# Neighbourhood attention, first steps: order of GpSimd's sorts, a half tile filled by ScalarE, and a 384-column pass for V

## The chip, the cores and the metric

The kernel runs on one core of a Trainium2 chip. The metric is the device time of one execution in microseconds (us); a kernel's time is the median of its runs. In the profile PE is TensorE's matmul stream and PEld its weight loads, DVE is VectorE, ACT is ScalarE, POOL is GpSimd and SP is SyncE, which here only issues DMAs. L12 is line 12 of the kernel.

## The reference

The image is 224 x 224 pixels of 192 channels in bf16. Every pixel attends to a 7 x 7 window with a distance of 2 between neighbours, clipped at the borders:

```python
qkv = x @ wqkv
q, k, v = (qkv[..., :C], qkv[..., C:2 * C], qkv[..., 2 * C:])
...
logits = jnp.einsum('bnc,bnkc->bnk', qf, kn) * C ** (-0.5)   # kn: the 49 neighbours' keys
p = _softmax(logits, axis=-1)
o = jnp.einsum('bnk,bnkc->bnc', p, vn) @ wo
```

Because of the distance of 2, pixels of odd and even rows never meet, nor do those of odd and even columns: there are two row classes (rc 0 and 1) and two column classes (cc 0 and 1), each 112 pixels long.

## The kernel before

**Tiling.** There are 14 steps: 7 blocks of 16 rows (ti) by 2 row classes (rc), the class changing fastest. Step n has 7 pairs m of two slots, and a slot is 8 columns wide. So there are 98 pairs k, and the main loop runs over k. Key and query weights are multiplied together once (tiles aw), and so are value and output weights (tiles wp); the kernel then needs only two projections of x:

- G = x times aw, one "whole" item per column class and group of slots, and one "halves" item per group. ScalarE copies the latter out of PSUM as gx, and POOL copies gx into the second half of G (L456).
- V = x times wp, one V item per slot: `v_item` (L343), and `v_first` (L358) for seven items of row class 1 at the very start. An item is `v_mms` (L336): the 192 columns of each column class get a first pass over 128 channels and a second over the other 64, and each pass is two matmuls of 64 stationary columns (h = 0 and 1, which run side by side in the two column halves of the array). That is eight matmuls of 192 columns, with eight weight loads. The second pass of both classes reads the same stationary operand, at(1, h).

**Input.** x comes in 14 bands of 16 image rows. SP loads each band with three transposing DMAs (L154): k = 0 and k = 2 go to XA, k = 1 to a tile x1 of which there are two buffers, so the load of band 2's x1 waits until all readers of band 0's are done. Two copies (xb_items, L160) move x1 into XB, and three (sort_items, L170) rearrange a band into the tile XS, from which the V items read. In the start VectorE does the copies of bands 0 and 1 (L366, L160, L170), POOL the sort of band 1; later bands are copied by POOL. The V items made in step 1 (for step 2) need the sort of band 3, those made in step 2 that of band 4.

**A pair** runs through stage1 (scores s, L497; row maximum nmx on VectorE, L499), stage1b (exp on ScalarE, p, L507), stage2 (transposes of p on TensorE, L526, copied out by VectorE, pt_sb, L527), stage3 (o_ps = p times V, L536) and stage4 (VectorE divides by the row sum, L542 and L559, and DMAs go out). Stages 3 and 4 are those of the pair two before. V lies in two tiles: VF, and VD, which has the partition halves swapped and is filled from VF by DMAs (vd_high, vd_low). In step 0 the lower half of VD[0] meets only weights that are zero, so what it holds need only be finite.

**The order.** The order of each engine's instructions is that of the program (in_order, L89). Between the pairs' stages the main loop puts the next step's G items (gw, gh) and V items (vs). In step 0 it also has to finish step 0's own: the lists in L658 give each pair's items, and L703 says which of them VectorE copies out instead of ScalarE. POOL has a queue pool_q: the sorts and xb copies of a coming band are put at its head in given pairs (L727 to L738), DMAs that write the first slot's result (L588, fifteen or ten for a step) are appended at its end, and each pair takes four entries from it (pool_do, L748). POOL's gx copies and the out DMA in L569 are issued where they stand, so they come before that pair's four entries. In step 0 the sort of band 3 for class 0 is put in at pair 5; in step 1 that of band 4 for class 1 at pair 4.

Of the kernel before, what the change touches and what calls it, by code (L numbers as in the profile page):

```python
# [8 lines left out]
BF = mybir.dt.bfloat16  # L9
# [12 lines left out]
NSLOT = 14  # L22
NSTEP = 14
NBAND = 14
RP = 48
RW = 2 * S
MM = 16
BND = 16 * S
C = 192
# [69 lines left out]
def kernel(  # L99
# [189 lines left out]
    LAY = {(0, 0): (0, 128, 0), (0, 1): (128, 64, 0), (1, 0): (64, 128, 0), (1, 1): (0, 64, 64)}  # L289
    AW, WP = {}, {}  # L290
    for key, (c0, cn, p0) in LAY.items():
        AW[key] = pers.tile([128, C], BF, name="aw%d%d" % key)
        WP[key] = pers.tile([128, C], BF, name="wp%d%d" % key)
        if cn < 128:
            z = 64 - p0
            nc.gpsimd.memset(AW[key][z:z + 64, :], 0.0)
            nc.gpsimd.memset(WP[key][z:z + 64, :], 0.0)
# [14 lines left out]
    for which in range(2):  # L312
        for key in ((0, 0), (1, 0), (0, 1), (1, 1)):
            (c0, cn, p0) = LAY[key]
            pt = ps_g.tile([128, 512], F32, name="prA", tag="pg")
            for d in range(2):
                nc.tensor.matmul(pt[p0:p0 + cn, 0:C], lhsT=wT[:, 2 if which else 0, d, c0:c0 + cn], rhs=wo_in[:, d, :] if which else wT[:, 1, d, :], start=(d == 0), stop=(d == 1))
            if which:
                nc.scalar.copy(out=WP[key][p0:p0 + cn, :], in_=pt[p0:p0 + cn, 0:C])
            else:  # L320
                nc.scalar.mul(AW[key][p0:p0 + cn, :], pt[p0:p0 + cn, 0:C], scale)
    setup_cm.__exit__(None, None, None)

# [11 lines left out]

    def v_mms(pv, at):  # L336
        for cc in range(2):
            for pas in range(2):
                for h in range(2):
                    k = 1 if pas else 2 * cc  # L340
                    nc.tensor.matmul(pv[64 * h:64 * h + 64, cc * C:(cc + 1) * C], lhsT=at(k, h), rhs=WP[(cc, pas)][:], start=(pas == 0), stop=(pas == 1))  # L341

# [260 lines left out]

    act, dve, pool = nc.scalar.copy, nc.vector.tensor_copy, nc.gpsimd.tensor_copy
    pool_q = []
    end_q = []
# [10 lines left out]
    g_row(0, 0, 1, 3, pool, first0)  # L617
    g_col(0, 0, 4, 10, pool)
    for it in load_items(2):
        it()  # L620
    for it in first_sort(dve) + xb_items(0, dve) + xb_items(1, dve) + sort_items(0, 0, dve):
        it()
    for j in range(7):
        v_first(j)(False)

    t = ps_t.tile([128, 8, 128], BF, name="pt_ps", tag="pt")
    for q in range(32):
        nc.tensor.transpose(t[64 * (q % 2):64 * (q % 2) + 64, q // 2 % 8, :], ident[:, 64 * (q % 2):64 * (q % 2) + 64], ident[:])
    sort1 = sort_items(1, 0, pool)
    for it in sort1[2:] + sort1[:2]:  # L630
        it()
    gw0, gh0 = g_all(0)
# [8 lines left out]

    for (c0, c1) in ((7, 14), (0, 7)):
        nc.scalar.dma_start(out=VD[0][0:64, c0:c1, 0:VP - 1], in_=VF[1][0:64, 7:14, 0:VP - 1])
    v0 = [v_item(0, cb) for cb in (13, 0, 1, 2, 3, 4, 5, 6, 7, 8, 9, 10, 11, 12)]
    ld = []

    for k in range(NP + 2):
# [3 lines left out]
        if J:  # L651
# [5 lines left out]
            if n == 0:  # L657
                w128 = (v0[:9] + gw0[2:4], v0[9:] + gw0[4:6], gw0[6:8] + vs[0:3], gw[0:2] + vs[3:6], gw[2:4] + vs[6:9], gw[4:6] + vs[9:12], gw[6:8] + vs[12:])[m]  # L658
                w64 = (gh0 + gh)[m + 1:m + 2]
# [4 lines left out]
            stage1(J, 1)  # L664
            if k == 0:
                marks(1, MM, 2 * MM, dve)
            stage1b(J, 0)
# [19 lines left out]

        first = n == 0 and k >= 2
        if k >= 2 and not first:
            stage4(pairs[k - 2], 1)  # L690
# [9 lines left out]
        if ld:  # L700
            ld.pop(0)()
        for i, it in enumerate(w128):
            it(n == 0 and (i in (0, 3 if m == 2 else 4) if first else i % 2 == 1))  # L703
            if n == 0 and it is v0[6]:
                vd_high(0, 13, 14)
                vd_high(0, 0, 6)
            if n == 0 and it is v0[13]:
                vd_high(0, 6, 13)
            if first and i == 0:
                stage4(pairs[k - 2], 1)  # L710
            if k == 1 and i == 1:
                xb2.pop(0)()
            if it is vs[6]:
                vd_high(rc1, 0, 7, nc.scalar if n == 0 else nc.sync)
            if it is vs[13]:
                vd_high(rc1, 7, 14, nc.scalar if n == 0 else nc.sync)
        if n == 0 and m == 0:
            xb2.pop(0)()
            for q in range(2):
                marks(q, 2 * MM, 2 * MM + 3, pool)  # L720
# [7 lines left out]
        if n == 0:  # L728
            add = {0: sort_items(1, 1, pool), 1: sort_items(2, 1, pool), 3: sort_items(2, 0, pool), 5: xb_items(3, pool) + sort_items(3, 0, pool)}.get(m, [])
        else:  # L730
            if m == 0 and n + 2 < NBAND:
                add = sort_items(n + 2, J.rc, pool)

            if m in (2, 4) and n + 3 < NBAND:
                srt = sort_items(n + 3, J.rc, pool)
                one, two = xb_items(n + 3, pool) + srt[2:], srt[:2]
                add = (two if m == 4 else one) if n > 1 else one + two if m == 4 else []
        pool_q[:0] = add  # L738
# [44 lines left out]
```

## Time and profile before

| what | value |
|---|---|
| median of three runs | 361.81 us (361.01 to 361.9) |
| the profiled execution's own time | 360.78 us |
| its span, from first to last instruction | 359.0 us |
| PE busy | 332.3 us (93%), 8120 matmuls |
| DVE busy | 314.3 us (88%) |
| ACT busy | 308.5 us (86%) |
| POOL busy | 283.0 us (79%) |
| mean granted TensorE clock | 0.996 |

The page's second part cuts the span into 40 equal slices, 9 us each; a digit is the busy share in tenths:

```profile
PE   4778997998999999999999999999999999999872
DVE  8977996997998989889989999799998989989893
POOL 8976899999896987969869699596995878374182
```

A 9 means 90% or more. PE has its low digits in the first eight slices and in the last three. So a mean over the span says little about the start.

The groups of instructions that the change touches, as the page gives them (busy us, mean ns of one, then idle time before them and what ended it):

```profile
L456 POOL COPY g<-gx 64x512 bf16<-64x512 bf16 (+1 forms) x110 | 62.1, 564 | 52.7 <-ACT gx L331 47.3
L341 PE MATMUL pv<-wp,xs 128*64 128x192 bf16 x1624 | 92.3, 249 | 11.7 <-DVE xs L366 3.6
L588 POOL DMA_DIRECT2D out_dram<-o_s x150 | 84.3, 569 | 9.0 <-DVE rs L542 7.8
L170 POOL COPY xs<-xa 128x896 bf16<-128x896 bf16 x52 | 47.4, 939 | 1.4
```

A matmul's duration (249 ns) is from issue to its modelled end; several are in flight at a time, so the pace is read from the starts of successive ones.

### The profile page before, as it was taken

What the parts mean: (1) busy time and instruction counts of PE and PEld (TensorE: products, weight loads), DVE (VectorE), ACT (ScalarE), POOL (GpSimd) and SP (SyncE); (2) the same over time, 40 slices, a digit from 0 to 9 for tenths busy, and PEclk for the clock granted to TensorE, in tenths of its full rate; (3) what the DMA queues carried; (4) which work ended last, traced back from release to release, by engine and by line L of the source; (5) the groups of instructions that cost most, each with busy time, mean ns of one, the idle gap of its engine ahead of it and who ended that gap; (6) DMA issues with size and microseconds to landing.
All of it is one profiled execution on the core that took longest, in us unless ns stands there. A gap on an engine that the chain in (4) does not pass through costs nothing.

```text
span 359.0 us, 19453 instructions
## 1 busy us (share of the span) xinstructions
PE 332.3 (93%) x8120; PEld 306.7 (85%) x8120; DVE 314.3 (88%) x741; ACT 308.5 (86%) x824; POOL 283.0 (79%) x448
## 2 busy tenths in 40 slices
PE   4778997998999999999999999999999999999872
PEld 2666876997999999999989998899999999999762
DVE  8977996997998989889989999799998989989893
ACT  6456776997999999999999998999999989999893
POOL 8976899999896987969869699596995878374182
PEclk9999999999999999999999999999999999999998
DMA  9999986899988989789898998988989855645424
GB/s 188 214 187 171 184 178 163 173 176 189 154 199 193 191 175 176 177 200 201 167 179 188 179 199 187 188 184 181 194 185 188 182 139 125 138 101 116 107 67 91
DMA packets 137539, 60.79 MB, mean 169 GB/s; under 512 B 88578, under 2 KB 136927, under 8 KB 137452
## 3 DMA queue, kind: packets, MB, share of 16 engines
q1 hardware_dynamic: 129124, 55.63, 78.0%
q10 hardware_dynamic: 3048, 2.23, 3.3%
q0 software_dynamic: 5280, 1.71, 2.9%
q8 instruction: 63, 1.03, 1.2%
q14 instruction: 24, 0.20, 0.2%
HBM read 0.29 MB, written 19.27 MB: 54 GB/s over the span
## 4 chain that ended last, share of the span: by engine, by line
PE 71%; POOL 12%; DVE 9%; ACT 4%; issue 2%; DMA 2%; DVEq 0%; ACTq 0%; POOLq 0%
PE s L497 15%; PE pv L341 15%; PE o_ps L536 15%; PE pg L421 10%; PE pt_ps L526 10%; PE pgh L421 5%; POOL out_dram L588 3%; POOL xs L170 3%; ACT p L507 2%; POOL g L456 2%; POOL xb L160 2%; DMA vd<-vf 2%; DVE xb L160 1%; DVE nmx L499 1%; POOL out_dram L565 1%
## 5 line engine op out<-in xcount | busy, mean ns | idle before, releaser
L507 ACT ACTIVATE p<-s,nmx 128x224 bf16<-128x224 f32 x392 | 149.7, 449 | 25.0 <-DVE nmx L499 21.5
L499 DVE TENSOR_REDUCE nmx<-s 128x2 f32<-128x392 f32 (+1 forms) x196 | 102.6, 564 | 19.8 <-PE s L497 18.4
L456 POOL COPY g<-gx 64x512 bf16<-64x512 bf16 (+1 forms) x110 | 62.1, 564 | 52.7 <-ACT gx L331 47.3
L341 PE MATMUL pv<-wp,xs 128*64 128x192 bf16 x1624 | 92.3, 249 | 11.7 <-DVE xs L366 3.6
L341 PEld LDWEIGHTS <-xs 128*64 128x64 bf16 x1624 | 78.7, 111 | 24.3 <-issue 7.6
L559 DVE TENSOR_TENSOR o_sb<-o_ps,rs 128x384 bf16<-128x384 f32 x169 | 94.2, 557 | 5.9
L331 ACT CAST vf<-pv 128x384 bf16<-128x384 f32 x193 | 87.3, 519 | 11.5 <-PE pv L341 9.4
L588 POOL DMA_DIRECT2D out_dram<-o_s x150 | 84.3, 569 | 9.0 <-DVE rs L542 7.8
L497 PE MATMUL s<-xa,g 128*64 128x196 bf16 (+6 forms) x990 | 82.8, 233 | 1.6 <-DVE g L329 0.8
L536 PE MATMUL o_ps<-vd,pt_sb 128*64 128x193 bf16 x784 | 81.8, 246 | 2.4 <-ACT pt_sb L527 2.1
L497 PE MATMUL s<-xb,g 128*64 128x196 bf16 (+7 forms) x990 | 82.3, 232 | 0.6 <-DVE g L329 0.4
L536 PE MATMUL o_ps<-vf,pt_sb 128*64 128x193 bf16 x784 | 81.8, 246 | 0.0
L497 PEld LDWEIGHTS <-g 128*64 128x64 bf16 x1980 | 78.2, 110 | 4.1 <-issue 2.0
L536 PEld LDWEIGHTS <-pt_sb 128*64 128x64 bf16 x1568 | 71.6, 109 | 4.0 <-ACT pt_sb L527 3.2
L527 DVE COPY pt_sb<-pt_ps 128x1024 bf16<-128x1024 bf16 x92 | 63.1, 686 | 5.9 <-PE pt_ps L526 0.8
L526 PE MATMUL pt_ps<-ident,p 128*64 128x128 bf16 x1552 | 63.9, 219 | 0.0
L526 PEld LDWEIGHTS <-p 128*64 128x64 bf16 x1552 | 57.3, 110 | 4.7
L331 ACT CAST g<-pg 128x512 bf16<-128x512 f32 (+4 forms) x136 | 57.5, 468 | 2.4 <-PE pg L421 2.2
L421 PEld LDWEIGHTS <-aw 128*64 128x64 bf16 x1320 | 55.5, 110 | 3.9 <-issue 0.6
L421 PE MATMUL pg<-xb,aw 128*64 128x512 bf16 (+9 forms) x440 | 54.5, 269 | 0.2 <-DVE xb L160 0.2
L421 PE MATMUL pg<-xa,aw 128*64 128x512 bf16 (+9 forms) x440 | 52.8, 270 | 0.1
L170 POOL COPY xs<-xa 128x896 bf16<-128x896 bf16 x52 | 47.4, 939 | 1.4
(73 smaller groups left out, 281.3 us busy)
## 6 DMA issues: line engine op xcount, KB each, us to landing
vd<-vf SPq DMA_DIRECT2D x47, 336.9 KB
out_dram<-o_sb SPq DMA_DIRECT2D x156, 96.0 KB
vd<-vf ACTq DMA_DIRECT2D x4, 336.9 KB
out_dram<-o_s POOLq DMA_DIRECT2D x78, 9.0 KB, 3.7
out_dram<-o_sb SPq DMA_DIRECT2D x13, 78.0 KB
out_dram<-xs SPq DMA_DIRECT2D x13, 78.0 KB
vd<-vf SPq DMA_DIRECT2D x2, 337.8 KB
xa<-in_x_dram SPq DMA_TRANSPOSE x28
```

Of the source, the lines that this page charges most:

```text
L331: nc.scalar.copy(out=out_, in_=in_)
L341: nc.tensor.matmul(pv[64 * h:64 * h + 64, cc * C:(cc + 1) * C], lhsT=at(k, h), rhs=WP[(cc, pas)][:], start=(pas == 0), stop=(pas == 1))
L421: nc.tensor.matmul(o, lhsT=l, rhs=r, start=(pas == 0), stop=(pas == 1))
L456: nc.gpsimd.tensor_copy(out=G[rc][cc][p:p + 64, 1, s0:s0 + ns, :], in_=gx[p:p + 64, 0:ns * 128].rearrange("p (s q) -> p s q", q=128))
L497: nc.tensor.matmul(o, lhsT=w, rhs=r, start=(pas == 0), stop=(pas == 1))
L499: nc.vector.tensor_reduce(out=nmx[:], in_=_win(s_ps, 0, 128, lo, [[256, 2], [16, 14], [1, 16 - lo]]), axis=AX.XY, op=ALU.max, negate=True)
L507: nc.scalar.activation(out=J.p[:, ab, cc, :, z:z + 112].rearrange("p q (r k) -> p q r k", k=8), in_=_win(s_ps, 0, 128, cc * 256, [[8, 2], ...
L526: nc.tensor.transpose(pt_ps[64 * h:64 * h + 64, 4 * ab + 2 * cc + q, :], J.p[:, ab, cc, q, 64 * h:64 * h + 64], ident[:])
L527: (nc.scalar.copy if J.n == NSTEP - 1 and J.m < 5 else nc.vector.tensor_copy)(out=J.pt[:], in_=pt_ps[:])
L536: nc.tensor.matmul(o_ps[64 * h:64 * h + 64, cc * 193:cc * 193 + 193], lhsT=J.pt[:, 4 * ab + 2 * cc + q, 64 * h:64 * h + 64], rhs=V[h][:, ( ...
L559: nc.vector.tensor_tensor(out=o_sb[:], in0=_win(o_ps, 0, 128, 0, [[194, 2], [1, C]]), in1=rs[:].unsqueeze(2).to_broadcast([128, 2, C]), op ...
L588: pool_q.append(lambda dst=dst, p=p, m=n * nj, cc=cc: nc.gpsimd.dma_start(out=dst.rearrange("j i c -> i j c"), in_=o_sb[p:p + m, cc, :]))
```

## The change

1. **V's second pass.** The two tiles for the second pass become one tile WB of 2 x 192 columns, and `v_mms` runs the second pass first, as one matmul of 384 columns per half h, and then the first pass of each class into its 192 columns. An item has six matmuls and six weight loads instead of eight and eight.
2. **VD's half.** The two DMAs that filled the lower half of VD[0] from VF[1], issued on ScalarE's queue, are gone. ScalarE fills it with one copy of a broadcast column (64 partitions x 14 x 385) after the weights' copies.
3. **The start.** Of the three sort copies of band 1 for class 0, VectorE takes k = 1 and k = 0 and POOL keeps k = 2. The copy of the border marks of XB[1] (L233) moves on VectorE from behind the first pair's maxima to before the first G copies. On POOL the two G column fills (L256, 32 x 1280) move behind the sort copy.
4. **POOL's queue.** The copies of band 3 are put into pool_q at pair 4 of step 0 instead of pair 5, those of band 4 at pair 3 of step 1 instead of pair 4. In POOL's order four DMAs of L588 that stood before the last sort copy of band 3 now stand behind it, and with them the gx copies and the out DMA of one pair; of those before the last sort copy of band 4, four DMAs now stand behind it, while the pair of gx copies that stood before that band's copies now stands between its second and its last sort copy.
5. **The lists** of step 0 are written as a table PLAN. On VectorE, ScalarE, SP and TensorE it gives the same order of items as before.

```diff
+    WB = pers.tile([128, 2, C], BF, name="wb")
     for key, (c0, cn, p0) in LAY.items():
-        WP[key] = pers.tile([128, C], BF, name="wp%d%d" % key)
+        WP[key] = pers.tile([128, C], BF, name="wp%d%d" % key)[:] if cn == 128 else WB[:, key[0], :]
...
+    nc.scalar.copy(out=VD[0][0:64, :, 0:VP - 1], in_=E[0:64, 0:1].unsqueeze(2).to_broadcast([64, NSLOT, VP - 1]))
...
     def v_mms(pv, at):
+        for h in range(2):
+            nc.tensor.matmul(pv[64 * h:64 * h + 64, 0:2 * C], lhsT=at(1, h), rhs=WB[:].rearrange("p t c -> p (t c)"), start=True, stop=False, skip_group_check=True)
         for cc in range(2):
-            for pas in range(2):
-                for h in range(2):
-                    k = 1 if pas else 2 * cc
-                    nc.tensor.matmul(pv[64 * h:64 * h + 64, cc * C:(cc + 1) * C], lhsT=at(k, h), rhs=WP[(cc, pas)][:], start=(pas == 0), stop=(pas == 1))
+            for h in range(2):
+                nc.tensor.matmul(pv[64 * h:64 * h + 64, cc * C:(cc + 1) * C], lhsT=at(2 * cc, h), rhs=WP[(cc, 0)], start=False, stop=True, skip_group_check=True)
...
-    g_col(0, 0, 4, 10, pool)
     for it in load_items(2):
         it()
     for it in first_sort(dve) + xb_items(0, dve) + xb_items(1, dve) + sort_items(0, 0, dve):
         it()
+    srt = sort_items(1, 0, dve)
+    srt[2]()
+    srt[0]()
+    marks(1, MM, 2 * MM, dve)
+    sort_items(1, 0, pool)[1]()
+    g_col(0, 0, 4, 10, pool)
...
-    sort1 = sort_items(1, 0, pool)
-    for it in sort1[2:] + sort1[:2]:
-        it()
...
-    for (c0, c1) in ((7, 14), (0, 7)):
-        nc.scalar.dma_start(out=VD[0][0:64, c0:c1, 0:VP - 1], in_=VF[1][0:64, 7:14, 0:VP - 1])
...
-            if k == 0:
-                marks(1, MM, 2 * MM, dve)
...
-            add = {0: sort_items(1, 1, pool), 1: sort_items(2, 1, pool), 3: sort_items(2, 0, pool), 5: xb_items(3, pool) + sort_items(3, 0, pool)}.get(m, [])
+            add = {0: sort_items(1, 1, pool), 1: sort_items(2, 1, pool), 3: sort_items(2, 0, pool), 4: xb_items(3, pool) + sort_items(3, 0, pool)}.get(m, [])
...
-            if m in (2, 4) and n + 3 < NBAND:
+            if m in ((2, 4) if n > 1 else (3,)) and n + 3 < NBAND:
                 srt = sort_items(n + 3, J.rc, pool)
                 one, two = xb_items(n + 3, pool) + srt[2:], srt[:2]
-                add = (two if m == 4 else one) if n > 1 else one + two if m == 4 else []
+                add = (two if m == 4 else one) if n > 1 else one + two
```

## The prediction

> **What bounds the kernel now.** I read the stretches first. Each row gives length, busy time of PE, PEld, DVE, ACT and POOL with instructions in brackets, clock, DMA share and GB/s:
>
> ```profile
> 10.00:20.00 10.00, 7.55 (x162) 6.71 (x162) 9.87 (x17) 4.27 (x15) 9.62 (x14) 1.00 1.21 199
> 20.00:30.00 10.00, 7.96 (x176) 6.72 (x177) 6.89 (x15) 5.21 (x13) 6.51 (x13) 1.00 1.18 197
> 56.00:61.00 5.00, 2.66 (x75) 2.45 (x71) 2.95 (x7) 2.34 (x10) 4.90 (x8) 1.00 0.69 166
> 82.00:86.00 4.00, 2.72 (x65) 2.28 (x66) 2.00 (x7) 2.61 (x10) 3.94 (x7) 1.00 0.88 190
> 86.00:220.00 134.00, 133.84 (x3356) 125.92 (x3352) 122.09 (x291) 125.65 (x337) 113.17 (x158) 1.00 0.94 184
> ```
>
> From 86 to 220 us PE is idle for 0.16 us in all, so whatever is gained earlier stays gained. Before that, PE loses time in three places: between 10 and 30 us, at 56 to 61 and at 82 to 86. In the first VectorE is full, in the other two POOL is. The chain of waits (start, duration, what) says the same:
>
> ```profile
> 16.88 2.39 DVE xs L170 x3
> ...
> 59.32 0.93 POOL xs L170
> ...
> 82.07 2.69 POOL xs L170 x3
> 84.76 0.04 issue
> 84.80 0.68 PE pv L341 x11
> ...
> 91.21 0.46 PE pg L421 x4
> 91.67 0.66 PE pv L341 x16
> ```
>
> From 43.09 to 84.76 us the chain stays on POOL, with gaps of at most 0.5 us: TensorE waits at 60.31 and 84.80 for POOL's last sort copy. The last two lines give paces: two matmul pairs of 512 columns take 0.46 us, eight pairs of 192 take 0.66. The timeline has the durations:
>
> ```profile
> 11.61 5.24 DVE L160 COPY xb<-x 64x1792 bf16<-64x1792 bf16 x4
> 16.88 2.04 DVE L170 COPY xs<-xa 128x896 bf16<-128x896 bf16 x2
> 18.84 0.42 DVE L170 COPY xs<-x 128x896 bf16<-128x896 bf16 x1
> 28.47 0.62 DVE L160 COPY xb<-x 64x1792 bf16<-64x1792 bf16 x1 [0.68 <-DMA x<-in_x_dram]
> 11.98 3.12 POOL L256 COPY g<-ch 32x1280 bf16<-32x1280 bf16 x2
> 19.29 2.60 SPq L154 DMA_TRANSPOSE x<-in_x_dram  x1
> 60.31 0.77 PE L341 MATMUL pv<-wp,xs 128*64 128x192 bf16 x13 [2.34 <-POOL xs L170]
> ```
>
> The same VectorE copy takes 0.62 us when POOL is idle and up to 1.58 in a row of four while POOL copies; a sort copy takes 0.42 against 1.0 to 1.1. The starts alternate: each VectorE copy waits for about one POOL copy.
>
> **The start, a gain of 1.0 us.** After: POOL finishes its row fills at 11.9 as now and then waits for band 1's k = 2 load. TensorE's first matmul that needs it starts at 16.49 after a step of 0.23 us, so I put the landing at 16.45. Until then VectorE is alone. From 11.61: four xb copies at 0.65 with their gap end at 14.2; five sorts (three as now, two new) at 0.45 end at 16.5. The marks copy (L233, 1.07 us at 21.79, moved ahead) then finds POOL's sort (0.93) asking first: 16.5 + 0.9 + 1.0 = 18.4, against 19.19, when the first G copy starts now: 0.8 earlier. TensorE's G matmuls end at 17.4 to 18.2 already. If POOL alternates twice before the marks (landing before 16.1), it is 19.5, 0.3 later than now; if the marks come first, 17.5, 1.7 earlier. I take 18.4, since the landing lies nearest to it.
>
> Behind the first maxima (20.80) the marks no longer stand, so VectorE copies its first V item 1.5 us earlier, but ScalarE, which waits for the maxima, gains 0.8 and shares the PSUM buffers; I take 1.0 at the second pair's maxima (29.01). The end values become -0.2 and 1.9.
>
> That needs band 2's x1, which VectorE waits for at 28.47, with the second pair's maxima queued behind it on VectorE. Its load is issued at 19.29, right behind VectorE's last sort of band 0 (19.26), which ends at 15.6 after; then SP's own queue ends at 17.68, so 1.6 earlier. And from 22 to 24 us the DMA view has nothing but the queue of the VD fills:
>
> ```profile
> q10 hardware_dynamic: 418, 0.31, 105.8%
> ```
>
> The two fills (0.66 MB) disappear. The load should land by 24, so it does not bind; if it came as late as now, the start would gain nothing, as in the lower end.
>
> **VD's fill on ScalarE, nothing.** No row has 5390 elements per partition. ScalarE's bf16 copies take 1018 ns for 1024 elements (L527) and 480 for 384 (L311), so 0.84 ns each: 4.7 us. The upper bound takes 480/384 = 1.25 ns: 6.7 us. It starts when the weights' copies end, at 8.20, and ScalarE is idle until 12.47. At 4.7 it ends 0.4 late; the seven V copies behind it, at 0.44 back to back (1.74 for four), end at 16.0 as now (16.13). At 6.7 they end at 18.0, 0.6 past the first G copy (17.38), which VectorE's 18.4 hides. If VectorE gained its full 1.7, the 0.6 would show.
>
> **POOL's queue, a gain of 2.3 us.** *First stall.* Ahead of band 3's last sort copy (59.32 to 60.25) four DMAs (48.1 to 50.4, 2.30), one pair of gx copies and an out DMA (57.48 to 59.28, 1.86 with gaps) disappear: it ends at 56.1, where TensorE arrives at 57.64. The 2.34 vanish, with 1.5 to spare. *Second stall.* TensorE now arrives earlier, but POOL has been busy without a gap since 43.09, and all that leaves its queue ahead of band 4's last sort copy is four DMAs: 4 x 0.568 (L588) = 2.27. So 84.75 becomes 82.5, and TensorE resumes 2.3 earlier than now. The second stall does not shrink: it lasts 2 us as before, because the arrival moved as far. The bounds: 1.7, if the DMAs' own idle gaps stay, and 2.34 + 2.0 = 4.3, if POOL found other time and both stalls went. I take 2.3, as POOL's rows add up to it. POOL's stretch itself begins behind a VectorE result (its out DMA waits for o_sb, 38.07), so the 1.0 of the start adds.
>
> What now comes later on POOL: gx copies of pair 5, done at 54.6 instead of 51.65, feed slots 6 to 9 of step 1, read at 67; out DMAs up to 3 us later, whose o_sb buffers (six) are written again at 61.5 at the earliest, after landing near 58.3 (3.6 us, as the others). After the second stall POOL is 2.3 behind relative to TensorE; it idles 0.73 at 91.5 and 3.12 at 113.9, and band 5's sorts (done at 103.1) are needed at 107.0. Uncovered, that lag would cost at most 2.3, which is the case of no gain.
>
> **The 384-column pass, a gain of 0.4 us.** Pairs of 192 go at 82.4 ns (0.66/8), which is 80 ns plus 2.4 if I compare with the 128-column transposes (0.45/8 = 56): slope 0.41 ns a column. A pair of 384 is then 162 where two pairs of 192 take 165. 203 items, some 180 of them in the full stretch: 180 x 2.4 ns = 0.4. The worst row is the 512-column pair, 230 ns, 0.449 a column: 172, a loss of 180 x 7.6 = 1.4. I take the first, since the 512-column reads are strided rows of x and WB is contiguous, like wp.
>
> [...]
>
> **Sum.** 1.0 + 2.3 + 0.4 = 3.7. On the profiled execution, 360.78 with a span of 359.0, that is 357.1. The median of the runs is 1.03 higher, 361.81; I predict medians: 358.1.
>
> **Rivals.**
> 1. *The collision only moves.* POOL's sort and column fills now meet VectorE's sorts and marks; the start gains 0 instead of 1.0: 361.8 - 2.7 = 359.1. For it: strict alternation, and a landing that is only inferred. Against: POOL has no input before.
> 2. *Both POOL stalls go*, because POOL's queue has more slack than its unbroken chain shows: 361.8 - 1.0 - 4.3 - 0.4 = 356.1. Against: rows of POOL back to back for 41 us.
> 3. *It does not do what it says*: the stalls shift to step 2 or 3, where POOL makes up its lag late, and the start's gain waits for the load of band 2. Within 1 us of now, 361.3.
> 4. *The wide pass is slower.* One place, `v_mms`, 203 times. It decides from the point where it eats the other 3.3: 3.3 us / 180 = 18 ns an item, a 384 pair of 183 ns. If the pass had to drain before the accumulation behind it starts, an item would lose up to 249 - 82 = 167 ns: 180 x 0.167 = 30, giving 388. At half that, 373. Against: passes of pg and s already accumulate at once without a gap.
> 5. *Weight loads set V's pace.* Two of eight fewer at 41 ns: 180 x 0.082 = 15, so 346.
>
> **How the numbers follow.** Forecast 0.55, rival 1 0.18, 2 0.11, 3 0.08, 4 0.06, 5 0.02. A change of 0.3%, 1.1 us, is about what can be told from none, so faster means below 360.7: forecast, 1, 2 and 5, 0.86; same is rival 3, 0.08; slower is rival 4, 0.06. The range takes in rivals 1 and 2 and the unknown costs between: 355.8 to 360.4; what is left out is 4, 5 and 3.
>
> **What would show it.** The first G copy on VectorE near 18.4 and the four xb copies in some 2.6 us instead of 5.24; band 2's xb copy without a wait for its DMA; no wait of TensorE for POOL's sort before 61 us, and one of about 2 us still there at the start of step 2; eight pairs' worth of V (two items) at 0.65 us. Wrong would be: a second stall that is gone, a stall at a new place between 86 and 120, VectorE's first G copy after 19.2, or V items above 0.67.

## The result and the profile after

The changed kernel takes 359.44 us (median of 5 runs, 358.6 to 359.77), the kernel before 361.66 in the same rounds (5 runs, 361.01 to 361.9). The ratio is 0.9939, with a 95% interval of 0.991 to 0.9967: 2.2 us faster, where 3.7 were forecast. The profiled execution of the changed kernel took 359.52 us with a span of 357.8.

First the same stretches as before, from the windows of the changed kernel (length, busy time of PE, PEld, DVE, ACT and POOL, clock, DMA share, GB/s):

```profile
10.00:20.00 10.00, 7.98 (x151) 6.87 (x153) 8.06 (x22) 7.33 (x16) 5.38 (x7) 1.00 1.20 191
20.00:30.00 10.00, 8.31 (x161) 6.72 (x160) 7.38 (x12) 5.56 (x14) 7.76 (x18) 1.00 0.98 208
56.00:61.00 5.00, 4.02 (x113) 3.79 (x110) 3.72 (x11) 3.44 (x12) 4.94 (x10) 1.00 0.69 162
82.00:86.00 4.00, 3.45 (x77) 3.24 (x78) 2.88 (x7) 1.83 (x7) 4.00 (x8) 1.00 0.85 185
86.00:220.00 134.00, 131.65 (x3137) 121.74 (x3137) 119.96 (x287) 125.47 (x336) 113.38 (x158) 1.00 0.94 186
```

Between 56 and 61 us TensorE is busy for 4.02 instead of 2.66 us, between 82 and 86 for 3.45 instead of 2.72. VectorE is no longer full at the start. But from 86 to 220 us, where TensorE had been idle for 0.16 us, it is now idle for 2.35 (134.00 less 131.65).

The timeline of the changed kernel at the start (start, duration, engine, line, operation; in brackets the idle time before it and what ended it):

```profile
8.28 4.68 ACT L323 COPY vd<-e 64x5390 bf16<-64x5390 bf16 x1
11.61 2.72 DVE L160 COPY xb<-x 64x1792 bf16<-64x1792 bf16 x4
15.87 1.08 DVE L233 COPY xb<-xb 64x3584 bf16<-64x3584 bf16 x1
16.22 1.69 PE L644 MATMUL pt_ps<-ident 128*64 128x128 bf16 x32
18.75 0.62 DVE L331 CAST g<-pg 128x24 bf16<-128x24 f32 x4 [1.80 <-PE pg L423]
25.48 1.80 POOL L170 COPY xs<-xa 128x896 bf16<-128x896 bf16 x2
26.57 2.07 DVE L160 COPY xb<-x 64x1792 bf16<-64x1792 bf16 x1
27.24 0.93 POOL L170 COPY xs<-x 128x896 bf16<-128x896 bf16 x1
28.57 1.05 DVE L501 TENSOR_REDUCE nmx<-s 128x2 f32<-128x420 f32 x2
```

The four xb copies take 2.72 instead of 5.24 us, and VectorE is through with sorts and marks (its L233 copy) at 16.95. It then waits 1.80 us for TensorE. Later one xb copy of band 2 takes 2.07 us (0.62 before); it ends 0.5 us after the third of POOL's sorts, and the second pair's maxima stand behind it, at 28.57 (29.01 before).

The same timeline at the two former stalls, and at the start of step 7:

```profile
55.17 0.93 POOL L170 COPY xs<-x 128x896 bf16<-128x896 bf16 x1
56.91 0.60 ACTq L357 DMA_DIRECT2D vd<-vf  x1
57.56 0.79 ACT L509 ACTIVATE p<-s,nmx 128x224 bf16<-128x224 f32 x2 [2.02 <-DVE o_sb L561]
58.72 0.35 PE L340 MATMUL pv<-wb,xs 128*64 128x384 bf16 x2 [0.98 <-ACT gx L333]
81.56 0.93 POOL L170 COPY xs<-xa 128x896 bf16<-128x896 bf16 x1
82.55 0.27 PE L343 MATMUL pv<-wp,xs 128*64 128x192 bf16 x1 [1.08 <-POOL xs L170]
84.47 0.86 ACT L333 CAST vf<-pv 128x384 bf16<-128x384 f32 x2 [2.17 <-PE o_ps L538]
87.07 0.35 PE L340 MATMUL pv<-wb,xs 128*64 128x384 bf16 x2 [1.01 <-ACT g L333]
...
193.81 0.62 SPq L354 DMA_DIRECT2D vd<-vf  x1
198.69 0.86 ACT L333 CAST vf<-pv 128x384 bf16<-128x384 f32 x2 [1.11 <-DMA vd<-vf]
```

POOL's last sort of band 3 ends at 56.1, and TensorE no longer waits for it, but 0.98 us at 58.72 for a ScalarE copy. POOL's last sort of band 4 ends at 82.5 and TensorE waits 1.08 us. The last two lines show a wait that the prediction did not have: a step's first copy into VF stands still until an earlier DMA that reads those slots of VF (`vd_low`, issued 4.9 us earlier) has landed. At 84.47 the same wait stands in front of the same kind of copy, though the profile names TensorE: ScalarE waits there for the semaphore of the `vd_low` issued at 79.33, and the trace has the last of that DMA's sixteen semaphore updates at 84.40.

To follow the time I compare, between two traces, when the scores of each of the 98 pairs start on TensorE. A difference that stays is a gain kept; where it jumps, time went. The gain over the profiled execution of before, in us, for all kernels of this study, with the time of the profiled execution itself in the last column:

| kernel | step 0, pair 1 | step 0, pair 3 | step 1, pair 1 | step 2, pair 1 | step 2, pair 2 | last pair | span | time |
|---|---|---|---|---|---|---|---|---|
| changed kernel | 1.13 | 0.45 | 1.79 | 2.34 | 1.37 | 1.48 | 1.26 | 359.52 |
| POOL queue alone (e4) | 0.00 | -0.68 | 0.71 | 1.58 | 1.12 | -2.31 | -2.35 | 363.13 |
| order of the start alone (e5) | 1.21 | -0.46 | -0.47 | -0.44 | -0.44 | -0.50 | -0.54 | 361.32 |
| fill alone (e6) | 0.70 | 0.39 | 0.36 | 0.34 | 0.34 | -0.19 | -0.41 | 361.18 |
| wide pass alone (e7) | 0.01 | -0.28 | -1.28 | -1.16 | -1.16 | -1.46 | -1.45 | 362.23 |
| DMA issue to SP (e2) | 2.21 | -1.10 | 1.45 | 1.24 | 1.23 | 0.56 | 0.40 | 360.38 |
| VD's copies split (e3) | 2.08 | -1.12 | 1.43 | 1.22 | 1.22 | 1.45 | 1.50 | 359.28 |
| xb copies later (e9, e9 again) | 1.89, 1.88 | 1.80, 1.79 | 3.84, 3.57 | 4.03, 4.02 | 3.43, 4.01 | 2.86, 3.24 | 2.67, 3.16 | 358.11, 357.62 |
| TensorE busy early (e11) | 0.30 | -0.80 | 1.04 | 1.53 | 1.14 | 1.38 | 1.15 | 359.63 |
| xb later and split (e8) | 1.98 | 1.90 | 4.45 | 4.23 | 4.23 | 3.74 | 3.83 | 356.95 |
| band 4's xb on VectorE (e13) | 1.00 | 0.91 | 2.95 | 3.20 | 3.20 | 1.93 | 2.01 | 358.77 |
| old order, xb later (e10) | 0.68 | 0.58 | 0.09 | 0.50 | 0.49 | -2.49 | -2.59 | 363.37 |

Pairs are counted from 0, so pair 1 is a step's second. Each kernel has one profiled execution here (e9 two), and apart from the changed kernel, e8 and e9 again it has one time in all. The executions of the kernel before took from 360.5 to 367.1 us beside these runs, so that a difference of one microsecond between two single times says little; where in the trace it arises says more.

### The profile page after: what moved, and what is told of

It is laid out like the page before. It is cut to its first block, busy times and chain, and to the rows that moved or that the text cites. A ratio compares the mean times of both kernels' runs of the same rounds, so it can differ in the third digit from the quotient of the medians.

```text
span 357.8 us, 18637 instructions
## 1 busy us (share of the span) xinstructions
PE 332.1 (93%) x7714; PEld 301.9 (84%) x7714; DVE 312.2 (87%) x743; ACT 313.7 (88%) x825; POOL 280.0 (78%) x446
## 3 DMA queue, kind: packets, MB, share of 16 engines
q0 software_dynamic: 5280, 1.71, 2.8%
## 4 chain that ended last, share of the span: by engine, by line
PE 71%; ACT 8%; DVE 7%; POOL 6%; DMA 3%; issue 2%; ACTq 0%; DVEq 0%; SPq 0%; POOLq 0%
PE s L499 15%; PE o_ps L538 14%; PE pg L423 10%; PE pt_ps L528 9%; PE pv L340 9%; PE pv L343 8%; PE pgh L423 6%; ACT p L509 5%; DMA vd<-vf 3%; POOL out_dram L590 2%; POOL xs L170 2%; DVE nmx L501 1%; ACT vf L333 1%; POOL xb L160 1%; POOL g L458 1%
## 5 line engine op out<-in xcount | busy, mean ns | idle before, releaser
L501 DVE TENSOR_REDUCE nmx<-s 128x2 f32<-128x392 f32 (+1 forms) x196 | 102.6, 565 | 18.4 <-PE s L499 16.0
L499 PE MATMUL s<-xa,g 128*64 128x196 bf16 (+7 forms) x990 | 82.3, 233 | 1.2 <-ACT p L509 0.5
L340 PE MATMUL pv<-wb,xs 128*64 128x384 bf16 x406 | 72.7, 334 | 10.5 <-DVE xs L368 3.9
L343 PE MATMUL pv<-wp,xs 128*64 128x192 bf16 x812 | 73.1, 250 | 1.1 <-POOL xs L170 1.1
L343 PEld LDWEIGHTS <-xs 128*64 128x64 bf16 x812 | 59.7, 112 | 10.0 <-POOL xs L170 1.3
L423 PEld LDWEIGHTS <-aw 128*64 128x64 bf16 x1320 | 54.6, 110 | 3.2
```

What stands on the lines that cost most here:

```text
L340: nc.tensor.matmul(pv[64 * h:64 * h + 64, 0:2 * C], lhsT=at(1, h), rhs=WB[:].rearrange("p t c -> p (t c)"), start=True, stop=False, skip_g ...
L423: nc.tensor.matmul(o, lhsT=l, rhs=r, start=(pas == 0), stop=(pas == 1))
L499: nc.tensor.matmul(o, lhsT=w, rhs=r, start=(pas == 0), stop=(pas == 1))
L501: nc.vector.tensor_reduce(out=nmx[:], in_=_win(s_ps, 0, 128, lo, [[256, 2], [16, 14], [1, 16 - lo]]), axis=AX.XY, op=ALU.max, negate=True)
```

## The experiments

### The four parts, each alone in the kernel before

**POOL's queue.**

```diff
-add = {... 5: xb_items(3, pool) + sort_items(3, 0, pool)}.get(m, [])
+add = {... 4: xb_items(3, pool) + sort_items(3, 0, pool)}.get(m, [])
-if m in (2, 4) and n + 3 < NBAND:
+if m in ((2, 4) if n > 1 else (3,)) and n + 3 < NBAND:
-    add = (two if m == 4 else one) if n > 1 else one + two if m == 4 else []
+    add = (two if m == 4 else one) if n > 1 else one + two
```

> The kernel before with the change's POOL queue alone (bands 3 and 4 one pair ahead, slot 0's stores behind them). Theory: the queue is worth what it is worth in the changed kernel. The start stays as before (second pair's first scores within 0.1 us of before), TensorE's 2.34 us wait for POOL's band-3 sort goes and 1.0 us of it comes back as ScalarE's DMA issue standing ahead of its copy of p, and POOL's last band-4 sort copy ends some 2.2 us earlier, near 82.5; then the copy of VF at the start of step 2 waits about 1 us for the earlier VD copy to land. Gain at the second pair of step 2: 1.9 us, left at the third: 0.9 to 1.9; time 359.9 to 360.8. Rival: POOL's stretch is tied to the start, so that without the earlier sorts of band 1 the queue gains less than 1 us at the second pair of step 2.

From pair 3 of step 0 to pair 1 of step 2 it gains 1.58 + 0.68 = 2.26 us. The theory's pieces are there: 0.92 us of waiting for gx at 59.80, 0.95 for POOL at 83.23, 0.49 for ScalarE at 87.31. The same difference in the table is 1.89 for the changed kernel, 2.34 for e2 and e3, 2.23 for both profiles of e9, 2.33 for e8 and e11; in e5, e6 and e10, with the old queue, it is 0.02, -0.05 and -0.08, and in e7 -0.88, by a loss in step 0 that is told below. So the queue is worth 1.9 to 2.3 us wherever the start lies, and the rival falls. One figure shows why: in all profiles but that of e13, pair 1 of step 2 starts 0.41 us (with the wide pass) or 0.49 to 0.50 us (without) after POOL's last sort copy of band 4 ends, whether that is at 80.6 us (e8) or at 86.0 (e7). What follows after 86 us in this execution (3.9 us lost again by the end) comes mostly in jumps at pair 1 of steps 2, 3, 5 and 11 and at pair 4 of step 8. Its time, 363.13 where 359.9 to 360.8 was expected (364.54 for the kernel before beside it), was therefore missed.

**The order of the start.**

```diff
     g_row(0, 0, 1, 3, pool, first0)
-    g_col(0, 0, 4, 10, pool)
...
+    srt = sort_items(1, 0, dve)
+    srt[2]()
+    srt[0]()
+    marks(1, MM, 2 * MM, dve)
+    sort_items(1, 0, pool)[1]()
+    g_col(0, 0, 4, 10, pool)
...
-    sort1 = sort_items(1, 0, pool)
-    for it in sort1[2:] + sort1[:2]:
-        it()
...
-            if k == 0:
-                marks(1, MM, 2 * MM, dve)
```

> The kernel before with the new order of band 1's sorts at the start alone (POOL idle beside VectorE's copies); the fill stays two DMAs, V stays four passes of 192. Theory A (TensorE's pace set the start of the changed kernel): here TensorE's first matmul starts at 10.8 as before, its matmul pairs go from 160 to 82 ns near 14.6 as before, the G matmuls start near 16.3 and VectorE's first G copy follows its marks at once, at 17.0 to 17.4 (18.75 in the changed kernel): the second pair's first scores come 1.8 to 2.5 us earlier than before. Theory B (copies of POOL and VectorE collide): TensorE is early all the same, but VectorE is not: first G copy at 18.4 or later, second pair 1.1 us earlier at most.

The second pair's scores came 1.21 us earlier, the third pair's 0.46 later. Neither theory had the reason, which one line of its timeline shows:

```profile
28.93 0.62 DVE L160 COPY xb<-x 64x1792 bf16<-64x1792 bf16 x1 [2.35 <-DMA x<-in_x_dram]
```

VectorE waits 2.35 us for band 2's load, ahead of the second pair's maxima. In the four profiles with VD's fill as two DMAs (before, e4, e5, e7) that copy starts at 28.5 to 29.1 and has waited 0.7 to 2.4 us for the load. In the kernels without these DMAs the first such copy has no wait for the load. So the new order alone leaves nothing at the third pair until the DMA fill is gone. Between theories A and B this run doesn't decide, as the condition of A was not met: pairs ran at 160 ns until 17.0 us here too, though TensorE had started at 10.84, and VectorE's first G copy, at 18.43, came behind G matmuls that began at 17.42.

**The fill.**

```diff
+    nc.scalar.copy(out=VD[0][0:64, :, 0:VP - 1], in_=E[0:64, 0:1].unsqueeze(2).to_broadcast([64, NSLOT, VP - 1]))
-    for (c0, c1) in ((7, 14), (0, 7)):
-        nc.scalar.dma_start(out=VD[0][0:64, c0:c1, 0:VP - 1], in_=VF[1][0:64, 7:14, 0:VP - 1])
```

> The kernel before with VD's unused half filled by ScalarE alone. Theory A (the fill is hidden): the fill takes 4.7 us and ends near 12.9, the first copy of V comes 0.5 us late, TensorE's pairs still go from 160 to 82 ns near 14.6, since three PSUM buffers cover it, the G matmuls start within 0.2 us of before, and the first scores within 0.2 us. Theory B (the fill holds TensorE back, which then reaches its full pace late): pairs at 160 ns until after 16, G matmuls start 1 us or more later, first scores 0.5 to 1 us later.

The signs of theory B came: pairs ran at 160 ns until 16.5, the G matmuls started at 17.35 instead of 16.23, the first scores 0.54 us later. But its cause is not shown, since pairs also stayed at 160 ns until 17.5 in e4 and 17.0 in e5, which keep the DMA fill. And there was no effect behind it: VectorE's first G copy and the first maxima stand where they stood (19.20 and 20.81). The third pair gained 0.39 us and kept it to step 2 (0.34): nearly the 0.45 of the whole change, with the old order of the sorts. One xb copy of band 2, no longer waiting for its load, sets that place, as in the changed kernel:

```profile
27.00 1.70 DVE L160 COPY xb<-x 64x1792 bf16<-64x1792 bf16 x1
28.62 1.05 DVE L500 TENSOR_REDUCE nmx<-s 128x2 f32<-128x420 f32 x2
```

**The wide pass.** As in the change, `WB` and the new `v_mms`, nothing else.

```diff
+        for h in range(2):
+            nc.tensor.matmul(pv[64 * h:64 * h + 64, 0:2 * C], lhsT=at(1, h), rhs=WB..., start=True, stop=False, ...)
         for cc in range(2):
-            for pas in range(2):
...
```

> The kernel before with the 384-column pass of V alone. Theory A (the order of the passes holds the start back): the wide pass reads band 0's last sort, so TensorE's first matmul starts at 11.7 instead of 10.8, and its pairs reach the full pace only near 17.5 (14.6 before): G matmuls start 1 us or more later; from step 2 on 4 to 5 ns a pair are won, 0.35 us in all; time 361 to 362.5. Theory B (the late full pace of the changed kernel came from elsewhere): full pace near 14.6, start within 0.2 us of before, time 360.3 to 361.3. [...]

The first matmul started at 11.73, full pace came at 14.9 and the first scores at 17.95 as before: theory A falls. The drift of some 0.005 us a pair is there (from -1.16 to -1.07 between pair 2 of step 2 and pair 1 of step 5). The rest of its loss, 1.26 us at pair 4 of step 0 and jumps at steps 5 and 7, lies at places where waits vary between executions; its cause was not looked for further. The time, 362.23, tells nothing between the two theories.

### Inside the changed kernel

**ScalarE's DMA issue.**

```diff
-        "Hd:6 N- Ha:7 Wa:12 Wa:13 Ta:7:14",
+        "Hd:6 N- Ha:7 Wa:12 Wa:13 T-:7:14",
```

In PLAN a word is one item of a pair: V and W are V items for steps 0 and 1, G and H likewise G items, X the next xb copy of band 2, R and T the DMAs of VD's upper half, N the second half of stage 4. The letter behind it is the engine that copies out or issues: a for ScalarE, d for VectorE; for R and T, - is SP.

> The changed kernel with the last copy of VD's upper half in step 0 issued by SyncE instead of ScalarE. Theory: that DMA issue, waiting in ScalarE's queue ahead of the copy of p, is what TensorE waits for at 58.72 (0.98 us, for gx). Without it the wait is below 0.3 us and the second pair of step 1 starts 0.7 to 1.0 us earlier than in the changed kernel. But POOL's last band-4 sort copy still ends near 82.5, since POOL's chain does not hang on it: TensorE's wait there grows from 1.08 to some 2 us, and the gain at the second pair of step 2 stays at 2.3 us: the total does not move (359.0 to 360.0). Rival: POOL's stores wait for results of the pairs, so that POOL's chain comes earlier with them, and the 0.7 to 1.0 us stay to the end (358.5).

TensorE has no such wait between 53 and 66 us, as expected, and the gain from pair 3 of step 0 to pair 1 of step 1 is 2.55 instead of 1.34 us. To pair 1 of step 2 it is 2.34, so 0.45 is left of the 1.21. But the next run, e3, has the issue in ScalarE's queue as the changed kernel, and shows 2.55 and 2.34 as well. The traces tell why. The issue waits for a semaphore that it shares with a store of o_sb. In the changed kernel this store was issued at 53.77 and its last update came at 56.84; the VD issue followed at 56.91, and p, whose first maxima were done at 56.11, at 57.56. In e3, which came 1.6 us late out of step 0, the store had landed at 55.99; the issue was through at 57.73, and p followed at 57.78, 0.1 us after its maxima. So the issue does hold p back in the changed kernel, by 1.4 us, and half of that is the store ahead of it.

And this wait doesn't matter at step 2: e4 gains 1.39 us to pair 1 of step 1 and 2.26 to step 2, e9 2.04 and 2.23, e2 and e3 2.55 and 2.34. POOL's chain evens it out. Two expectations failed: in e2 POOL's last sort of band 4 ends at 83.60 instead of near 82.5, as its start was late, and the wait for it is 0.71 us, not 2; just before, TensorE waits another 0.79 us for VectorE, which has waited 2.12 us for a store. The time, 360.38, is above the expected 359.0 to 360.0.

**VD's lower copies split.**

```diff
         if 0 < n and m == 5 and n + 2 < NSTEP:
-            vd_low(J.rc, 0, 7)
+            vd_low(J.rc, 3, 7)
+        if 0 < n and m == 3 and n + 2 < NSTEP:
+            vd_low(J.rc, 0, 3)
```

> The changed kernel with each copy of VD's lower half (slots 0 to 6, issued at pair 5 of a step) split: slots 0 to 2 at pair 3, slots 3 to 6 at pair 5. Theory: ScalarE's first copy into VF of a step waits for the landing of that DMA, and this is the 0.97 us lost between the second and third pair of step 2, and the 0.2 to 1.0 us lost at the same place of steps 5 and 7. With the split these are gone: the gain of 2.3 us at the second pair of step 2 stands at the third and to the end, apart from the wide pass; time 357.5 to 358.6. Rival: the wait is for something else (a PSUM buffer, a store), then the same 0.5 to 1 us steps stay at steps 2, 5 and 7 and the time is 359.0 to 360.0.

I take the smallest time of each pair over all kernels of the study as its undisturbed time. Above it, the pairs 1 of steps 2 to 13 lose 0.25 us in all here, and 0.24 in e8, which has the split too. The third kernel with the split, e13, loses 1.9, but 1.63 of it at step 9, where VectorE waits 1.33 us for a store of o_sb; no copy into VF waits more than 0.2 us for a VD DMA at pair 1 in any of the three. In the other profiles the pairs 1 lose 2.6 (changed kernel), 1.4 (before) and 1.2 to 3.9, except e5 with 0.1. But three other pairs now lose some 0.4 us each, and at the first of them the profile names such a DMA, that of slots 7 to 13:

```profile
90.29 1.13 SPq L354 DMA_DIRECT2D vd<-vf  x1
...
95.64 0.48 ACT L333 CAST vf<-pv 128x384 bf16<-128x384 f32 x1 [1.12 <-DMA vd<-vf]
```

So the cause of the waits is right, and the remedy moves part of them. The time, 359.28, is the rival's and not the 357.5 to 358.6 of the theory. Its start, 1.57 us behind the changed kernel at pair 3 of step 0, is told below under the clock.

**Band 2's xb copies later.**

```diff
-        "Va:0 ... Vd:7 Va:8 Gd:2 Ga:3 X-",
-        "Va:9 Vd:10 X- Va:11 Vd:12 Va:13 R-:6:13 Gd:4 Ga:5",
+        "Va:0 ... Vd:7 Va:8 Gd:2 Ga:3",
+        "Va:9 Vd:10 X- Va:11 Vd:12 Va:13 R-:6:13 Gd:4 X- Ga:5",
```

> The changed kernel with band 2's two xb copies on VectorE moved behind the second pair's maxima (the first stood ahead of them and took 2.07 us instead of 0.62 beside POOL's sorts). Theory: the second pair's maxima start at 27.2 to 27.9 instead of 28.57, the third pair's scores start 0.7 to 1.4 us earlier than in the changed kernel, and the lead is still there at the second pair of step 2; time 358.0 to 358.8. Rival: the copies meet POOL's sorts just as badly later on (2 us again), or ScalarE's V copies set the second pair's place: less than 0.3 us at the third pair.

The second pair's maxima start at 26.80, earlier than the theory's range, and the lead over the changed kernel is 1.35 us at pair 3 of step 0 and 1.69 at pair 1 of step 2. The timeline of the repeated run:

```profile
25.53 1.81 POOL L170 COPY xs<-xa 128x896 bf16<-128x896 bf16 x2
26.81 1.07 DVE L501 TENSOR_REDUCE nmx<-s 128x2 f32<-128x420 f32 x2 [0.92 <-PE s L499]
27.28 0.93 POOL L170 COPY xs<-x 128x896 bf16<-128x896 bf16 x1
29.12 0.73 DVE L160 COPY xb<-x 64x1792 bf16<-64x1792 bf16 x1
```

The maxima, which read PSUM, run in 1.07 us beside POOL's sorts, and the xb copy behind them takes 0.73. Part of the lead is TensorE's earlier full pace in this execution (15.8 us against 17.5): e13, with the same edit and full pace at 17.7, has its maxima at 27.70 and leads the changed kernel by 0.46 at pair 3.

**TensorE busy early.** The 32 transposes stand ahead of the first V items and are 72.

```diff
-    for j in range(7):
-        v_first(j)(False)
-    (32 transposes of ident)
+    (72 transposes of ident)
+    for j in range(7):
+        v_first(j)(False)
```

> The changed kernel with the 32 idle transposes between the first V items and the first G moved ahead of the first V items and made 72, so that TensorE is busy from 7.8 us on while it waits for x. Theory (TensorE's late full pace held the start back): the first V items' matmul pairs run at full pace from their start or from 14.5 at the latest (17.6 in the changed kernel), the G matmuls start at 15.3 to 16.2 instead of 17.74, VectorE's first G copy right behind its marks, at 17.0 to 17.3 instead of 18.75, the first scores at 17.3 to 18.0 instead of 18.89; the third pair's scores 0 to 1 us earlier, as band 2's xb copy allows. Rival: ScalarE's fill and its seven V copies set the start, G matmuls start no earlier than 17.2.

The V items ran at full pace from 12.0 us and G started at 15.38, as the theory has it, and then this line ended it:

```profile
17.99 0.22 PE L423 MATMUL pg<-xa,aw 128*64 128x39 bf16 x2 [2.38 <-DMA xa<-in_x_dram]
```

The G matmuls behind the first need a load that in this execution landed at 18.0 (POOL's first sort, which waits for band 1's load, started at 18.07, against 16.38 in the changed kernel). The first scores came at 19.30, 0.41 later than in the changed kernel. The third pair came 1.25 us behind the changed kernel, where 0 to 1 us ahead was expected: band 2's xb copy, from 27.40 on, again ended 0.5 us behind POOL's third sort, at 29.89. So TensorE's slow start is not the only bound: the load is the next, and how much it binds on other executions this run doesn't tell.

**Old order, xb copies later.** The kernel before with the fill on ScalarE (as in e6), and:

```diff
-            if k == 1 and i == 1:
+            if k == 1 and i in (1, 5):
                 xb2.pop(0)()
...
         if n == 0 and m == 0:
-            xb2.pop(0)()
```

> The kernel before with VD's fill on ScalarE and band 2's xb copies behind the second pair's maxima: band 1's sorts and marks stay in their old order. Theory A (the new order of the sorts is worth what the prediction gave it, about 1 us): the second pair's maxima start 0.8 us or more later than the 26.80 of the same kernel with the new order: 27.6 to 28.2. Theory B (the gain of the start is the fill's and the xb2 copy's; the order gives nothing): 26.6 to 27.1.

The second pair's maxima start at 28.02, against 26.80 with the new order (e9): theory A, and full pace, at 15.1 here and 15.7 there, can't be the reason. But the worth of the order hangs on it. With the old order VectorE's first G copy starts at 19.2 in all five profiles (before, e4, e6, e7, e10), whether full pace came at 14.6 or at 17.5. With the new order it follows TensorE: 17.7 (e2, full pace at 14.9) to 18.9 (e13, at 17.7). And e13, with its late pace, has the second pair's maxima at 27.70, only 0.3 us ahead of the old order. So the new order is worth 0.3 to 1.2 us at the second pair, once the xb copy is out of the way. (e9 also has the wide pass and POOL's new queue, which alone moved the second pair's scores by 0.01 us or less.)

**Band 4's xb copies on VectorE,** on top of xb later and split:

```diff
-                one, two = xb_items(n + 3, pool) + srt[2:], srt[:2]
+                one, two = (xb_items(n + 3, pool) if n > 1 else []) + srt[2:], srt[:2]
+        if n == 1 and m in (2, 3):
+            xb_items(4, dve)[m - 2]()
```

> As the xb2 and split version, with band 4's two xb copies taken from POOL and given to VectorE in step 1 (pairs 2 and 3). Theory A (a VectorE copy that meets a run of POOL copies waits until the run ends, as at 26.6 and 25.5 us, not for one POOL copy only): at least one of the two takes 1.5 us or more instead of 0.62, its pair is late by 1 us or more, and the total is no better than without it although POOL's last band-4 sort copy ends 1.5 us earlier. Theory B (they alternate, as I wrote in the prediction): 0.6 to 1.6 us a copy, the second stall at the start of step 2 shrinks by 0.8 us or more, and the total is 0.5 to 1.3 us better.

```profile
66.06 0.62 DVE L160 COPY xb<-x 64x1792 bf16<-64x1792 bf16 x1 [0.87 <-DMA x<-in_x_dram]
...
69.60 0.88 DVE L160 COPY xb<-x 64x1792 bf16<-64x1792 bf16 x1
70.51 1.04 DVE L501 TENSOR_REDUCE nmx<-s 128x2 f32<-128x392 f32 x2
71.11 0.79 ACT L509 ACTIVATE p<-s,nmx 128x224 bf16<-128x224 f32 x2 [1.22 <-DVE nmx L501]
```

The copies took 0.62 and 0.88 us, as theory B has it (no run of sorts stood beside them). The wait for POOL at step 2 is gone. But ScalarE waits 1.22 us for the maxima behind the copies, and pairs 3 and 4 of step 1 lose 1.8 us. From pair 3 of step 0 to pair 1 of step 2 it gains 2.29 us, against 2.33 in e8, the same kernel without this edit. Theory B's 0.5 to 1.3 us less did not come (358.77 in one execution). VectorE has no room there for what POOL can't do.

**The best of these, timed.** e9 again, and e9 with the split of e3.

> The changed kernel with band 2's xb copies moved behind the second pair's maxima, now timed in rounds. Theory: 1.0 to 1.7 us less than the changed kernel's 359.4, so 357.7 to 358.4. Rival: its single run was a lucky one for the places that vary (VD's landings, the half clock); then 358.8 to 359.6.

> The changed kernel with band 2's xb copies behind the second pair's maxima and VD's lower copies split over pairs 3 and 5. Theory: the start keeps its 1.4 to 1.8 us over the changed kernel, and the losses at the second pair of a step (0.2 to 1.3 us each, 1 to 3.5 us a run) stay below 0.2 us, so that it beats the xb2 edit alone by 0.5 to 1.5 us: 356.5 to 357.8, against 359.4 of the changed kernel. Rival: the split only moves the landing's wait to later pairs of a step (0.4 us each, as in the split alone): the same as the xb2 edit alone, 358.0 to 358.6.

The xb edit alone takes 358.32 us (12 runs), a ratio to the kernel before of 0.9899 with an interval of 0.9859 to 0.994. With the split it is 358.85 (6 runs), 0.9894 with 0.9834 to 0.9953. The changed kernel's interval, 0.991 to 0.9967, overlaps both: some 1.4 us better by the ratios, as expected, but not settled by these runs; the places in the traces speak for it. The split adds nothing that can be measured (356.5 to 357.8 was expected), and its rival holds: the waits reappear later in the step, at pair 4 of step 2 here, after a DMA issued at 87.30.

```profile
87.30 1.24 SPq L354 DMA_DIRECT2D vd<-vf  x1
...
92.89 0.48 ACT L333 CAST vf<-pv 128x384 bf16<-128x384 f32 x1 [1.26 <-DMA vd<-vf]
```

## Why the prediction held, and where its steps failed

The time lay inside the range, 1.3 us above the forecast. Its place there is partly luck: of the 3.7 us, the two traces show 1.26, and the medians are 2.2 apart because the profiled execution of before was a quick one. The terms fared as follows.

**The start: 1.0 forecast, 0.45 measured.** The four copies at 2.72 us were right. VectorE's five sorts took 1.5 us, not five times 0.45, so its marks did not find POOL's sort asking first: they began at 15.87, before POOL's sort, which started at 16.38, and ended at 16.95. The first G copy at 18.75 is near the 18.4 of the forecast only because TensorE came late; in e2, e3 and e9, with the same start, it is at 17.7 to 18.0. The step that failed is the one on band 2: "The load should land by 24, so it does not bind". The load didn't bind; the copy behind it did. It starts at 25.49 in e2, 25.62 in e3 and 26.57 in the changed kernel, and ends at 28.63 or 28.64 in all three, 0.5 us after POOL's third sort. So the second pair's maxima stand at 28.56 to 28.57 whatever was won before. The line for e2:

```profile
25.48 1.80 POOL L170 COPY xs<-xa 128x896 bf16<-128x896 bf16 x2
25.49 3.15 DVE L160 COPY xb<-x 64x1792 bf16<-64x1792 bf16 x1
27.23 0.93 POOL L170 COPY xs<-x 128x896 bf16<-128x896 bf16 x1
```

I had costed the collision at 11 to 19 us, where the change removes it, and not at the next place where VectorE copies. Rival 1, "the collision only moves", named the right mechanism, at another place; its 359.1 is closer to the result than the forecast. And the gain of the start was booked to the order, whereas e6 has 0.39 of the 0.45 from the fill alone: the same copy caps both.

**VD's fill: nothing, and so it was.** It took 4.68 us (4.7 forecast), and ScalarE's first V copy came at 12.99 instead of 12.47. The cover was TensorE itself, at 0.64 us an item, behind three PSUM buffers. In e11, where it was at full pace already, the cover was gone and it waited 0.85 us at 13.85 for ScalarE.

**POOL's queue: 2.3 forecast, 1.9 measured, 2.2 to 2.3 in the other runs.** POOL's copies ended at 56.1 and 82.5, as worked out. What the changed kernel lacks beside the others is one wait of POOL itself, for band 3's load, which landed at 48.07; in the other profiles with this queue it had landed before POOL came (idle 0.05 us there):

```profile
48.13 3.39 POOL L160 COPY xb<-x 64x1792 bf16<-64x1792 bf16 x2 [0.48 <-DMA x<-in_x_dram]
```

How it divides was wrong: the first stall does not vanish "with 1.5 to spare", as ScalarE's copy was late next, and the second is 1.08 instead of 2. The two faults cancel, for the reason given there: POOL's chain alone sets pair 1 of step 2.

**The wide pass: 0.4 forecast, some 0.35 by the traces.** Two V items go at 0.653 instead of 0.659 us, start to start in the steady stretch, and e7's drift over the 77 pairs from step 2 to step 12 makes 0.35; the time of one run can't show so little. Rivals 4 and 5 are out: two items are 0.006 us shorter, where a drain at its worst would have made them 0.33 longer and weight loads that set the pace 0.16 shorter.

**What the sum lacked.** "Whatever is gained earlier stays gained" was read from one execution that had 0.16 us of idle time after 86 us. The prediction named "a stall at a new place between 86 and 120" as a sign that it is wrong, and there is one, 1.01 us at 87.07: the VF copy at 84.47 behind VD's DMA, then G's copies behind it. Before, TensorE came to that place 2.3 us later, and no such wait shows there. Such waits occur in nearly all profiles at changing steps. What lies above the undisturbed times from pair 2 of step 2 on is 1.9 us in the kernel before, 1.7 in the changed one, and 1.6 to 5.3 in the others. The profiled execution of before was 0.9 us below its kernel's median, that of the changed kernel at its median, so that the spans differ by 1.26 us and the medians by 2.2.

## What to carry to other kernels

When an engine is freed of a collision, look where its next instruction of the same kind falls, and what stands behind that one: here the whole gain of the start ended at one copy ahead of the maxima. Where one engine's chain sets a checkpoint (POOL at step 2), cost the change by that chain alone; waits won or lost before it cancel. And "stays gained" needs more than one execution without idle time: the DMA that reads VF just before it is written again was hidden here only as long as its writer came late, and cost 1.01 us at 87.07 once TensorE came 2.3 us earlier.

## What the runs showed of the hardware

**A run of POOL copies can hold VectorE's copy until the run ends.** In five profiles (changed kernel, e2, e3, e6, e11) one xb copy of 0.62 us met three sorts of POOL, each of which starts 0.05 us before the end of the one ahead. Wherever it came in, it ended 0.47 or 0.48 us after the third sort, and took up to 3.15 us (e2, where it waited for one sort after the other). But a run doesn't always do this. In the kernel before, VectorE's copies took turns with POOL's copies from 11.6 us on (0.79, 1.58 and 1.56 us) and also with the sorts at 15.2 to 18.7 us, whose starts overlap by the same 0.05 us (1.25, 1.01 and 1.11 us). What decides between the two is open. The second pair's maxima on VectorE, which read PSUM, took 1.07 us beside such a run in the repeated e9, and 1.05 behind it in the changed kernel.

**TensorE's full pace comes at a moment that the kernel alone doesn't set.** With the same code at the start, pairs of matmuls went over from 160 to 82 ns at 17.5 us (changed kernel), 14.9 (e2), 15.4 (e3), 15.7 and 15.8 (both of e9) and 17.7 (e13). The earliest is 11.9, in e11, whose 72 transposes start at 7.79. The trace's record of the clock begins at just these moments (14.55 us in the kernel before, 17.53 in the changed one); the clock column, which has nothing to go by before, shows 1.00 there. Later it does show another kind of stretch; these are windows of e6, behind its stall of 2.36 us:

```profile
58.00:60.00 2.00, 0.05 (x2) 0.06 (x4) 0.60 (x2) 1.72 (x8) 1.96 (x4) 1.00 0.76 179
60.00:62.00 2.00, 2.00 (x36) 2.00 (x38) 0.71 (x2) 1.00 (x3) 1.97 (x4) 0.73 0.75 190
62.00:64.00 2.00, 2.00 (x40) 2.00 (x38) 1.22 (x4) 1.32 (x4) 1.93 (x4) 0.50 0.41 97
64.00:66.00 2.00, 2.00 (x44) 1.91 (x42) 1.28 (x3) 1.50 (x5) 2.00 (x3) 0.91 0.90 201
```

There the clock is granted at half for 3.41 us (1.7 us of clock lost). Of the five kernels with the old POOL queue four had it behind the first stall (e5, e6, e7, e10), at a price of 1.3 to 1.4 us in e5, e6 and e7 that POOL's stall at step 2 hid. In e2 and e3 it came between 32 and 36 us, and they leave pair 3 of step 0 1.6 us behind the changed kernel; in e11 it came at 18.8 to 22.2. The kernel before and the changed kernel had none in their profiled executions until 355.89 and 355.45 us; the last 3.1 and 2.3 us of their spans are at half.

In these traces the times between the recorded changes are multiples of 3.413 us: from full pace to half clock 6.83 (e11), 17.07 (e2, e3), 44.37 (e5, e6, e10) and 47.79 (e7) are 2, 5, 13 and 14 of them, and the 341.33 and 337.92 us at full clock of the kernel before and of the changed kernel are 100 and 99. So I counted windows of this length from the first record of each trace, up to 340 us. In all 14 profiles the seven windows in which TensorE was idle (by the modelled ends of its matmuls) for 1.99 (e3) to 2.48 us (e2) were followed by half clock, and none of those with 1.71 us (e11) or less was. This also fits the kernel before, which has no drop behind its stall of 2.34 us: the stall lay across two windows, with 0.96 and 1.38 us in them.

These are counts over 14 executions: what sets the moment of full pace, and what the 3.413 us come from, no run here shows.
